# A spectral filter and MLP kernel: the second transform step over pairs of groups, on array quarters

## The chip, the cores and the metric

The kernel runs on one core of one Trainium2 chip. The metric is device time in microseconds (us) of one execution. Engines are named as the profile names them: PE is TensorE's matmul, PEld its weight load, DVE is VectorE, ACT is ScalarE, POOL is GpSimd, SP is SyncE (which issues the DMAs here).

## The reference

Four layers on an activation x of 2048 rows by 640 columns, in fp32: a spectral filter, an MLP over the rows, and both again.

```python
x = x + _A_ref(_layernorm(x), A_w_r, A_w_i)
x = x + _B_ref(_layernorm(x), B_w1, B_b1, B_w2, B_b2)
x = x + _A_ref(_layernorm(x), A_w_r, A_w_i)
x = x + _B_ref(_layernorm(x), B_w1, B_b1, B_w2, B_b2)

def _A_ref(x, w_r, w_i):            # x: (1, 2048, 640), w: (2048, 321)
    X = rfft2(x, axes=(-2, -1)) * (w_r + 1j * w_i)
    return irfft2(X, s=(S, D), axes=(-2, -1))

def _B_ref(x, w1, b1, w2, b2):      # w1: (2048, 1728), w2: (1728, 2048)
    u = gelu(einsum("bsd,sf->bdf", x, w1) + b1)
    return (einsum("bdf,fs->bds", u, w2) + b2).transpose(0, 2, 1)
```

## The kernel before

Everything is one class, `Layers`, whose `run` calls for each of two rounds `a1` (filter, forward transform and product), `a2` (inverse transform, residual) and an MLP: `b1st` in the first round, `b2nd` in the second.

Nearly all matmuls are in fp16 at fp32-like precision: an operand is split into a high part (`h`, made on ACT by a copy to fp16) and a low part (`l`, what is left, mostly made on DVE). `mm3` issues three matmuls for one product: high by high, high by low, low by high.

The two-dimensional transform is done by tables. Along the 2048 rows it goes in two steps (2048 = 16 x 128). The first step over rows, `a0_s1f` or `a0_s1`, is done per row tile `j` of 16; its result is written by `a0_s1h` (ACT) and `a0_s1l` (DVE) into `s1h` and `s1l`, both [128, 80, 16, 8] fp16. In the first layer this is a stage of its own, which ends at some 60 us; in the second it runs beside the first MLP, with a tail `a0_tail` after the last row tile.

Then `a1` works on 16 groups `g` of 128 rows of frequencies, 321 columns each for real and imaginary part:

- `dstage(g)` (called D in the prediction): the transform along columns, with `s1h` and `s1l` as stationary operands and table `tD`. 24 matmuls of 160 or 161 columns for the first two groups, 16 for the others: these take the remainder of the columns from a tile `stk`, filled by DMA (`stack`) from a DRAM copy `rest` of a part of `s1h` and `s1l`.
- `psplit`: ACT makes `ph`, DVE `pl`, from PSUM.
- `s2stage(g)` (s2): the second step over rows, table `tS2` as stationary operand, [128, 128] fp16: 12 matmuls of 321 columns. The table is block-diagonal but for the order of its rows: rows of the input are ordered `j16 * 8 + c8`, and a row of `c8` feeds only the 32 outputs of slot `c8 // 2`.
- `product`: the spectrum times the filter's weights `w` (loaded by DMA, three buffers): DVE makes `ta` and `tb` from PSUM, POOL combines them into `ta`.
- `xsplit`: ACT makes `xh`, DVE `xl`, both scaled by `sx`, a scale per row that `scale_x` computes once, in the first layer, with two small matmuls and a chain of small DVE operations that ends in `ce`. `twice` then copies 63 columns to the tile's end, of `xh` on ACT and of `xl` on POOL.
- `is2stage(g)` (IS): the inverse of s2, 36 matmuls of 64 rows by 128 columns.
- `yevict` (ACT) writes two thirds to `Y` in fp32; `y2evict` (ACT) takes the last third to `yt`, and `y2split` makes `Y2h` and `Y2l` of it on POOL.

The order is written out by hand: `self.pin = True` keeps each engine (PE, DVE, ACT, POOL) to the order in which the program issues instructions, one iteration of the loop at line 584 for each group. In an iteration PE has D of group g+1, IS of g-3, s2 of g; DVE has the products of g-1, `pl` of g+1, `xl` of g-2. Iterations also carry parts of other stages: `wsplit` of the first MLP weight tile in quarters (ACT and DVE), its scan and scale, loads of `tDi`, `tIM` and the weights. The last two groups are issued after the loop, in thirds.

PSUM is one pool of four buffers of two banks each, [128, 2, 512] fp32, handed out in turn by `big()`.

In `b1st` the second product accumulates, for each row tile `j` of 16, over 14 tiles of the 1728 hidden rows. The last hidden tile has 64 rows. It is stored twice in the 128 rows, and `ul` holds the high part in its lower half and the low part in its upper half, so that one matmul with `wh` does for two; the matmul with `wl` then takes 64 rows only:

```python
mm(o, wh[:, ft], ul[ft][:, a], start=False, stop=False)
mm(o, wl[:64, ft], uh[ft][:64, a], start=False, stop=True)
```

## Time and profile before

| | us |
|---|---|
| median of 3 runs | 1049.42 |
| lowest and highest | 1048.08, 1050.31 |
| the profiled execution's own time | 1049.02 |
| its span, first to last instruction | 1047.2 |
| PE busy in the span | 1003.6 |
| DVE busy | 710.7 |
| ACT busy | 586.0 |
| POOL busy | 273.1 |

The lines of the profile read as follows. A timeline row has the start in us from the span's start, the time taken, the engine, the line (L49 is the wrapper through which all pinned operations go, so operations are told apart by their tiles), the operation, the tiles written and read, and the shape; in brackets, the idle time before it and what ended it. Rows that follow closely may be merged (x2). A group row has the count, the busy time and the mean of one in ns, and the idle time before. A row of a tile has the shortest, the median and the longest duration in ns, then the first and the last start. A row by stretch has the stretch, its length, the busy time and count of PE, PEld, DVE, ACT and POOL, the granted TensorE clock (1.00 is full), the share of DMA and GB/s. The stages in order: first step over rows to about 60 us, first filter stage to 134.5, inverse to about 200, first MLP to 568, second filter stage from 576 to 649, then the inverse and the second MLP.

### The profile page before, as it was taken

How to read it: one execution, taken by the hardware profiler on the slowest of the kernel's cores; microseconds unless marked ns; L12 is line 12 of the kernel's file. 1: busy time of each engine (PE TensorE's matmuls, PEld its weight loads, DVE VectorE, ACT ScalarE, POOL GpSimd, SP SyncE). 2: the span in 40 equal slices, each digit the busy share in tenths (PEclk: the TensorE clock that was granted, in tenths of full speed). 3: DMA queues.
4: the chain of work that ended last, by engine and by line, in shares of the span. 5: the costliest groups of instructions: out<-in, count | busy, mean ns of one | idle time of the engine just before them, and what ended most of it. 6: DMA issues, size and time to landing. Idle time of an engine off the chain costs nothing.

```text
span 1047.2 us, 20920 instructions
## 1 busy us (share of the span) xinstructions
PE 1003.6 (96%) x8315; PEld 732.1 (70%) x8315; DVE 710.7 (68%) x1437; ACT 586.0 (56%) x910; POOL 273.1 (26%) x481
## 2 busy tenths in 40 slices
PE   4889989999999999999998998999999999999998
PEld 3778756677777776777775786666777777777776
DVE  7978947854333955666665797677655574987885
ACT  5857669765555555555542475894644454644532
POOL 6927867300000002211122487770000000000000
PEclk9589989999999999999999998999999999999999
DMA  7864336622222264444423543464422232445511
GB/s 224 311 204 127 99 116 200 205 86 83 82 82 77 71 239 139 131 122 129 126 87 110 171 119 111 130 196 172 132 95 81 74 107 92 137 140 180 165 44 51
DMA packets 55305, 137.38 MB, mean 131 GB/s; under 512 B 6540, under 2 KB 12328, under 8 KB 55208
## 3 DMA queue, kind: packets, MB, share of 16 engines
q1 hardware_dynamic: 55208, 136.06, 41.1%
q8 instruction: 65, 1.06, 0.4%
q14 instruction: 32, 0.26, 0.1%
HBM read 112.96 MB, written 23.07 MB: 130 GB/s over the span
## 4 chain that ended last, share of the span: by engine, by line
PE 85%; DVE 8%; POOL 2%; DMA 2%; ACT 1%; issue 1%; SPq 0%; POOLq 0%; ACTq 0%; DVEq 0%
PE ps L49 85%; DVE f L49 2%; DVE s1l L49 1%; DVE hl L49 1%; DVE st L49 1%; DVE ta L49 1%; DVE xt L49 1%; DVE xl L49 1%; DMA xt<-x 1%; POOL eo L49 1%; DVE wl L49 0%; POOL ta L49 0%; DMA rest<-s1l 0%; DMA raw<-w 0%; DVE tb L49 0%
## 5 line engine op out<-in xcount | busy, mean ns | idle before, releaser
L49 PEld LDWEIGHTS <-wh 128*128 128x128 f16 x2992 | 289.9, 98 | 115.9 <-issue 2.0
L49 PEld LDWEIGHTS <-wl 128*128 128x128 f16 (+1 forms) x1616 | 157.8, 98 | 67.1 <-issue 4.2
L49 PE MATMUL ps<-hh,wh 128*128 128x320 f16 x896 | 186.3, 299 | 0.8 <-ACT hh L49 0.8
L49 PE MATMUL ps<-hl,wh 128*128 128x320 f16 x896 | 184.7, 299 | 0.0
L49 PE MATMUL ps<-hh,wl 128*128 128x320 f16 x832 | 171.4, 299 | 0.1
L49 DVE SCALAR_TENSOR_TENSOR wl<-raw,s,wh 128x1024 f16<-128x1024 f32 (+2 forms) x88 | 103.6, 1181 | 87.3 <-ACT wh L49 87.2
L49 PE MATMUL ps<-uh,wl 128*128 128x320 f16 x448 | 134.2, 300 | 0.0
L49 PE MATMUL ps<-ul,wh 128*128 128x320 f16 x448 | 133.7, 299 | 0.0
L49 ACT ACTIVATE wh<-raw,s 128x1024 f16<-128x1024 f32 (+2 forms) x92 | 94.8, 1048 | 67.7 <-PE ps L49 61.7
L49 PE MATMUL ps<-uh,wh 128*128 128x320 f16 x416 | 124.3, 299 | 0.0
L49 POOL TENSOR_TENSOR r<-v,mh 128x1 f32<-128x1 f32 x64 | 35.7, 559 | 330.1 <-DVE nm L49 314.6
L49 ACT ACTIVATE junk<-raw 128x896 bf16<-128x896 f32 (+1 forms) x60 | 59.6, 994 | 47.5 <-DMA raw<-w 47.3
L49 DVE TENSOR_TENSOR xt<-xt,ps 128x320 f32<-128x320 f32 (+1 forms) x96 | 44.9, 490 | 40.9 <-ACT ec L49 25.8
L49 PE MATMUL ps<-u,wo 128*128 128x320 f16 x504 | 69.9, 299 | 0.0
L49 DVE TENSOR_TENSOR f<-eo 128x256 f32<-128x256 f32 (+1 forms) x128 | 40.0, 366 | 41.8 <-POOL eo L49 41.2
L49 PEld LDWEIGHTS <-wo 128*128 128x128 f16 x504 | 49.3, 98 | 19.1
L49 DVE BATCH_NORM_STATS2 st<-xt 128x6 f32<-128x320 f32 x128 | 56.2, 481 | 5.0 <-DMA xt<-x 4.9
L49 PE MATMUL ps<-tM,f 128*128 128x128 f32 x160 | 40.5, 436 | 19.1 <-DMA xt<-x 11.8
L49 ACT ACTIVATE z<-xt,nb,r 128x640 f32<-128x640 f32 x31 | 28.5, 919 | 54.1 <-POOL z L49 43.7
L49 POOL TENSOR_TENSOR eo<-z 128x320 f32<-128x320 f32 x63 | 54.2, 881 | 17.0 <-ACT z L49 15.1
L49 PE MATMUL ps<-tDi,yh 128*128 128x322 f16 x256 | 56.6, 312 | 1.6 <-ACT yh L49 1.6
L49 PE MATMUL ps<-ph,tS 128*128 128x321 f16 (+2 forms) x288 | 57.9, 286 | 0.0
(165 smaller groups left out, 1904.3 us busy)
## 6 DMA issues: line engine op xcount, KB each, us to landing
raw<-w SPq DMA_DIRECT2D x56, 512.0 KB
xt<-x SPq DMA_DIRECT2D x80, 320.0 KB
w<-w SPq DMA_DIRECT2D x48, 321.0 KB
x<-xt SPq DMA_DIRECT2D x48, 320.0 KB
raw<-w SPq DMA_DIRECT2D x32, 448.0 KB
raw<-w2z SPq DMA_DIRECT2D x32, 448.0 KB
out<-xt SPq DMA_DIRECT2D x15, 320.0 KB
stk<-rest SPq DMA_DIRECT2D x42, 64.0 KB
```

The source lines that it names most:

```text
L49: i = f(*a, **k)
```

## The change

The second step over rows takes groups in pairs. The input rows are reordered to `c8 * 16 + j16`, which makes `tS2` block-diagonal in two blocks of 64. For the first 14 groups (`PG`), a product of 128 rows is replaced by one of the 64 rows of a half: `s2pair` issues, for a pair, 48 matmuls of 64 x 64 by 321 columns, four in a row on the four quarters of the array, for groups `e` and halves `r`. The result of half `r` of both groups lies in one PSUM tile, so that a "group" after s2 is now half of each of two old ones; `k_rows`, `gsel` and the places in `Y` follow. Group 14 still goes by `s2stage`, group 15 in thirds.

With it the loop goes by pairs, the splits are shared out anew (the scale `sx` moves into the product; ACT copies to `xh`; `xl` is made half on DVE and half on POOL; the copies to the tail columns go to DVE; `Y2h` goes from POOL to ACT), PSUM is split into three buffers and one, `w` gets a fourth buffer, and `scale_x` and the scales use spare columns of a PSUM tile in use. In `b1st` the matmul with `wl` takes 128 rows, the upper half of `uh` being set to zero.

```diff
-    def big(self):
+    def big(self, one=None):
+        if one is None:
+            self.turn += 1
+            one = self.turn % 4 == 0
+        tag, bufs = ("one", 1) if one else ("big", 3)
         self.n += 1
-        return self.psum.tile([128, 2, 512], F32, tag="big", name=f"ps{self.n}")
+        return self.psum.tile([128, 2, 512], F32, tag=tag, name=f"ps{self.n}", bufs=bufs)
...
-        self.s1h = p.tile([128, 80, 16, 8], F16, name=f"s1h{self.n}")
-        self.s1l = p.tile([128, 80, 16, 8], F16, name=f"s1l{self.n}")
+        self.s1h = p.tile([128, 80, 8, 16], F16, name=f"s1h{self.n}")
+        self.s1l = p.tile([128, 80, 8, 16], F16, name=f"s1l{self.n}")
...
-        self.T.activation(self.s1h[:, :, j], pv, AF.Copy, scale=S1S / (zs * TS))
+        self.T.activation(self.s1h[:, :, :, j], pv, AF.Copy, scale=S1S / (zs * TS))
...
         def y2evict(g, ps):
+            y2hi(g, ps)
             yt = self.t(p, [128, 2, 32, 4], F32, "yt", 2)
             T.activation(yt, pairs(ps, 256, 384), AF.Copy, scale=YS)
             return yt
         def y2split(g, yt):
-            G.tensor_copy(y2[0][:, g], yt)
-            G.tensor_tensor(y2[1][:, g], yt, y2[0][:, g], op=ALU.subtract)
+            for q in range(2):
+                G.tensor_tensor(lanes(self.Y2[1], g)[:, q], yt[:, q], lanes(self.Y2[0], g)[:, q], op=ALU.subtract)
...
+        def xhi(g, c, x):
+            T.activation(xs[g % 3][0][:, :, c], x, AF.Copy)
+        def xlo(g, c, x, r=slice(0, 2), e=V):
+            xh, xl = (q[:, r, c] for q in xs[g % 3])
+            e.tensor_tensor(xl, x[:, r], xh, op=ALU.subtract)
...
+        def s2pair(u, x):
+            ps = self.big(False), self.big(True)
+            for a, b in ((0, 0), (1, 0), (0, 1)):
+                for ri in range(2):
+                    for q in range(2):
+                        for e in range(2):
+                            for r in range(2):
+                                m = slice(64 * r, 64 * r + 64)
+                                sp = 1 if u == e == r == 0 else 0
+                                mm(
+                                    ps[r][64 * e:64 * e + 64, ri, :NL], self.tS2[m, a, sp, 2 * ri + q, m],
+                                    x[e][b][m, q, :NL], start=a == b == q == 0, stop=b == q == 1,
+                                )
+            return ps
...
+        def times(o, ps, g, w, c=slice(0, NL)):
+            n = c.stop - c.start
+            V.scalar_tensor_tensor(
+                o, ps[:, :, c], self.sx[:, g:g + 1], w[:, c].unsqueeze(1).to_broadcast([128, 2, n]),
+                op0=ALU.mult, op1=ALU.mult,
+            )
+        def product(g, ps):
             ta, tb = (self.t(p, [128, 2, NL], F32, a, n) for a, n in (("ta", 3), ("tb", 2)))
+            times(ta, ps, g, w[g][:, 0])
+            times(tb, ps, g, w[g][:, 1])
             G.tensor_tensor(ta[:, 0], ta[:, 0], tb[:, 1], op=ALU.subtract)
+            gi = G.tensor_tensor(ta[:, 1], tb[:, 0], ta[:, 1], op=ALU.add)
+            if g + 4 < NG:
+                w[g + 4] = wload(g + 4)
+            return ta, gi
...
+        def xfinish(g):
+            xlo(g, whole, ta.pop(g), slice(0, 1))
+            xh, xl = xs[g % 3]
+            V.tensor_copy(xh[:, :, NL:], xh[:, :, 257:320])
+            V.tensor_copy(xl[:, :, NL:], xl[:, :, 257:320])
...
+        for i in range(NG // 2):
+            a, b, k = 2 * i, 2 * i + 1, 2 * i - 4
+            pa = dstage(a)
+            pa = phi(pa) if i else pquarters(pa)
+            if k >= 0:
+                pv[k] = is2stage(k)
+                evict(k)
+            if i:
+                ta[a - 2], _ = product(a - 2, ps2.pop(a - 2))
+                if k >= 0:
+                    y2split(k, yt.pop(k))
+            if k >= 0:
+                xfinish(k + 1)
+            pb = d = dstage(b)
+            pb = phi(pb) if i else pquarters(pb)
+            stack(2 * i + 4)
+            if i:
+                pa = plo(*pa)
+                xhi(a - 2, whole, ta[a - 2])
+            if k >= 0:
+                pv[k + 1] = is2stage(k + 1)
+                evict(k + 1)
+            if i:
+                ta[a - 1], gi = product(a - 1, ps2.pop(a - 1))
+                xlo(a - 2, whole, ta[a - 2], slice(1, 2), G)
+                pb = plo(*pb)
+            if i < NG // 2 - 1:
+                ps2[a], ps2[b] = s2pair(i, (pa, pb))
+            else:
+                ps2[a] = s2stage(a, *pa)
+            if k >= 0:
+                y2split(k + 1, yt.pop(k + 1))
...
+            if first and i == 0:
+                for _ in self.scale_x(p, d):
+                    pass
+            if i:
+                if i < NG // 2 - 1:
+                    xhi(a - 1, whole, ta[a - 1])
+                    xlo(a - 1, whole, ta[a - 1], slice(1, 2), G)
+                xfinish(a - 2)
...
+            for q in {4: (0, 1), 5: (2,), 6: (3,)}.get(i, ()):
+                self.wsplit(0, quarter(q)[0], lo=False, part=quarter(q)[1])
+            if i > 3:
+                self.wsplit(0, quarter(i - 4)[0], hi=False, part=quarter(i - 4)[1])
...
             if ft == NFT - 1:
                 V.tensor_copy(ul[ft][:64], uh[ft][:64])
+                G.memset(uh[ft][64:], 0.0)
...
                     mm(o, wh[:, ft], ul[ft][:, a], start=False, stop=False)
-                    mm(o, wl[:64, ft], uh[ft][:64, a], start=False, stop=True)
+                    mm(o, wl[:, ft], uh[ft][:, a], start=False, stop=True)
...
-            r_in = j16 * 8 + c8
+            r_in = c8 * 16 + j16
```

Here `pquarters` makes the first two groups' splits by halves (ACT, then DVE, for each half), `phi` and `plo` are the ACT and the DVE part of the old `psplit`, `evict` is `yevict` and `y2evict`, and `lanes` gives the places in `Y` and `Y2` of a group after s2.

More of the change, by code (lines that the diff above doesn't have):

```diff
@@ L34 @@
 YS = 2.0 ** -14
+PG = 14
 I32 = mybir.dt.int32
@@ L101, in setup @@
         base = self.base = self.push("base", side="left")
-        self.psum = self.push("ps", bufs=4, space=PSUM)
+        self.psum = self.push("ps", bufs=1, space=PSUM)
+        self.turn = 0
         self.dram = self.push("dr", space=DRAM)
@@ L1570, in k_rows @@
             out[g, s * 32 + 16:s * 32 + 32] = b
+    half = out[:PG].reshape(PG // 2, 2, 2, 64)
+    out[:PG] = half.transpose(0, 2, 1, 3).reshape(PG, 128).copy()
     return out
```

190 lines of the change are left out of this document (83 added, 107 removed).

## The prediction

> **What bounds the kernel now.** I read the page's part 1 first, then the busy time by stage, then the order of instructions on each engine inside the filter stage (the timeline), then the groups. Part 1 of the page:
>
> ```profile
> span 1047.2 us, 20920 instructions
> PE 1003.6 (96%) x8315; PEld 732.1 (70%) x8315; DVE 710.7 (68%) x1437; ACT 586.0 (56%) x910; POOL 273.1 (26%) x481
> ```
>
> PE bounds the whole, but the shares average over stages. Busy time by stretch (PE, PEld, DVE, ACT, POOL): two stretches of the first filter stage, one of the first MLP.
>
> ```profile
> 80.00:88.00 8.00, 8.00 (x134) 6.57 (x130) 7.06 (x9) 6.21 (x15) 6.72 (x10) 1.00 0.42 121
> 112.40:121.00 8.60, 8.60 (x146) 6.87 (x142) 8.60 (x11) 5.89 (x13) 7.93 (x12) 1.00 0.55 156
> 330.00:560.00 230.00, 230.00 (x1777) 162.83 (x1776) 146.67 (x387) 119.62 (x174) 37.12 (x87) 1.00 0.39 126
> ```
>
> In the MLP (third row) PE has no gap and the rest lie well below it. The filter stage is another matter: per 8.00 us, which is two groups, DVE has 7.06 and POOL 6.72; where DVE also splits weights (second row), DVE is full. Time taken from PE there is worth at most what those two leave. PE's order within one group:
>
> ```profile
> 84.54 0.31 PE L49 MATMUL ps<-ph,tS 128*128 128x321 f16 x1
> 86.20 0.30 PE L49 MATMUL ps<-tD,s1h 128*128 128x160 f16 x2
> 87.44 0.28 PE L49 MATMUL ps<-tI,xh 64*128 64x128 f16 x4
> 88.55 0.31 PE L49 MATMUL ps<-ph,tS 128*128 128x321 f16 x1
> ```
>
> Second step (s2) 1.66, the next group's first step (D) 1.24, inverse step (IS) 1.11: 4.01 us. s2's pace, 0.138 for 321 columns, would give 55 ns for the 128 columns of an IS matmul of 64 rows; the 36 of them take 31 ns each, so two halves of the array do run side by side.
>
> DVE and POOL hold each other up. One group where DVE is full, and one xl that POOL left alone:
>
> ```profile
> 108.80 0.81 DVE L49 SCALAR_TENSOR_TENSOR pl<-ps,ph 128x642 f16<-128x642 f32 x1
> 109.53 0.74 DVE L49 SCALAR_TENSOR_TENSOR wl<-raw,s,wh 128x512 f16<-128x512 f32 x1
> 110.19 1.38 DVE L49 SCALAR_TENSOR_TENSOR xl<-ta,sx,xh 128x642 f16<-128x642 f32 x1
> 121.99 0.88 DVE L49 SCALAR_TENSOR_TENSOR xl<-ta,sx,xh 128x642 f16<-128x642 f32 x1
> ...
> 108.95 0.76 POOL L49 TENSOR_TENSOR ta<-ta,tb 128x321 f32<-128x321 f32 x1 [0.26 <-DVE tb L49]
> 109.67 1.21 POOL L49 TENSOR_TENSOR ta<-tb,ta 128x321 f32<-128x321 f32 x1
> 110.82 0.99 POOL L49 CAST Y2h<-yt 128x256 f16<-128x256 f32 x1
> ```
>
> The xl takes 1.38 and not 0.88, the second ta 1.21 and not 0.76; pl, which reads PSUM, is undisturbed. Read as a lock taken in turn between POOL and any DVE operation with two SBUF inputs, and held for some 0.15 to 0.18 less than the duration, the rows fit: wl frees it at 110.13; ta runs 0.75 from there to 110.88 and frees it at 110.70; xl runs 0.88 from there, to 111.58.
>
> **The change, part by part.** *MLP tile.* The end of one output tile on PE:
>
> ```profile
> 466.94 0.30 PE L49 MATMUL ps<-uh,wl 128*128 128x320 f16 x1
> 467.08 0.30 PE L49 MATMUL ps<-ul,wh 128*128 128x320 f16 x1
> 467.31 0.31 PE L49 MATMUL ps<-uh,wl 64*128 64x320 f16 x1
> ...
> 468.03 0.28 PE L49 MATMUL ps<-tM,fh 128*128 128x128 f16 x2
> ```
>
> Within one size a step is 0.14. From 467.08 to 468.03 lie four steps of 0.237, each into another size: a switch costs 0.10. At 128 rows none is left: 4 x 0.10 x 16 tiles = -6.5 us, where PE has no gap. The new memset of uh's upper half runs on a POOL that idles there, during the earlier matmuls of the first tile; uncovered it would cost its own length, once.
>
> *PE in the filter.* Per pair s2 goes from 24 matmuls to 12 steps of four quarters, 3.3 to 1.65 us, if the quarters run side by side as the halves of IS do. D and IS stay at 4.7, switches go from four to five: about 6.5 us a pair, not 8.0. PE alone would give -1.5 x 14 = -21 us; DVE and POOL decide what arrives.
>
> *DVE and POOL per pair.* The durations used:
>
> ```profile
> L49 DVE SCALAR_TENSOR_TENSOR xt<-ps,c,xt 128x640 f32<-128x640 f32 x16 | 14.1, 882 | 8.7 <-ACT xt L49 4.3 <-PE ps L49 4.2
> L49 DVE TENSOR_TENSOR fs<-f,fs 128x320 f32<-128x320 f32 x14 | 6.8, 488 | 0.2
> L49 DVE COPY f<-eo x32: 168/169/722, 12.5 to 573.2; 128x2 f32<-128x2 f32 x32
> 12.30 1.68 POOL L49 TENSOR_TENSOR eo<-z 128x320 f32<-128x320 f32 x2
> 132.41 0.72 POOL L49 TENSOR_TENSOR Y2l<-yt,Y2h 128x256 f16<-128x256 f32 x1
> L49 POOL TENSOR_TENSOR yl<-Y,yh 128x512 f16<-128x512 f32 x30 | 34.8, 1160 | 10.9 <-ACT yh L49 10.9
> ```
>
> The products now multiply by sx as well: 0.88 each, the next start 0.80 later (0.07 more than now). The V half of xl takes 0.49. The two tail copies take 0.2 each, an estimate from 0.17 for two elements. One copy of two elements took 0.72: the first, at 12.5, beside POOL's eo of 12.30. So copies queue for the lock too. POOL, by the line through 0.72 at 256 and 1.16 at 512: 0.84 for the G half of xl, 0.50 for each y2 half; the Y2h cast and the tail copy leave it. ACT loses the tail copy and gains Y2h (0.38, below): still some 6.4 a pair.
>
> The order matters more than the sums. Let T be the end of a pair's second product on DVE. POOL does both ta from T+0.07 to T+1.77 (the V half of xl takes a turn in between), then the G half of xl, to T+2.54. Only then may DVE copy xl's tail: the wait that the change adds. Behind it on DVE stand the next pair's products. POOL's first y2 half slips in ahead (T+2.48 against the copy's T+2.61), so the copy runs at T+2.82 and the next product from T+2.92 to T+4.60. Then V half and two copies alternate with ta (to T+5.6), then pl (to T+6.35) and the second product: T+8.03. The second copy and the second ta ask within 0.02 us of each other; if the copy loses, T+8.6. I take 8.2, between the two and nearer to the order as worked out. Now it is 8.0. s2 is no bound: it starts at T+0.1, ends by T+2.0 and is needed at T+2.9. PSUM neither: the second IS waits for pl's buffer until T+6.5 and ends by T+7.7, before the next s2 can start.
>
> *DMA.* w loads gain a buffer and go out a group earlier; stk still goes out a whole pair ahead; the weight and table loads move by a group at most. Queues are idle enough (DMA share 0.42 above): nothing, or the few tenths of a late stk.
>
> *Sum over the stages.* Rows of DVE that mark the end of pairs 0, 1 and 6 now, in the first layer and the second, the first product after them, and the scale of x (xq, ce):
>
> ```profile
> 66.24 0.39 PE L49 MATMUL ps<-eye,xq 128*16 128x128 f32 x2
> 68.93 0.17 DVE L49 TENSOR_REDUCE ce<-cx 128x1 f32<-128x16 f32 x1
> 72.69 0.81 DVE L49 TENSOR_TENSOR tb<-ps,w 128x642 f32<-128x642 f32 x1
> 79.13 0.82 DVE L49 TENSOR_TENSOR tb<-ps,w 128x642 f32<-128x642 f32 x1
> 120.53 0.81 DVE L49 TENSOR_TENSOR tb<-ps,w 128x642 f32<-128x642 f32 x1
> 123.40 0.83 DVE L49 TENSOR_TENSOR ta<-ps,w 128x642 f32<-128x642 f32 x1 [0.54 <-PE ps L49]
> 587.29 0.82 DVE L49 TENSOR_TENSOR tb<-ps,w 128x642 f32<-128x642 f32 x1
> 594.08 0.81 DVE L49 TENSOR_TENSOR tb<-ps,w 128x642 f32<-128x642 f32 x1
> 635.08 0.81 DVE L49 TENSOR_TENSOR tb<-ps,w 128x642 f32<-128x642 f32 x1
> ```
>
> Fill, first layer: s2 of pair 0 now also waits for group 1's split, four halves of some 0.5 on ACT and DVE in turn, which puts xq and ce 1.5 later. The products now need that scale: from 70.6 product, pl, product end at 74.6, now 73.5. Pair 1 follows 7.9 later (now 6.45): +2.5. Second layer, where stk's landing holds both kernels: +1.2. Five pairs: 5 x 8.2, three weight splits of 0.66, and in the first layer 1.0 for the weight scale: 44.0 against 41.4, and 43.0 against 41.0, so +2.6 and +2.0. Drain: the next product starts 3.6 after pair 6 (handoff and the fourth split), now 2.1; the six small products cost 0.06 more each; POOL has one y2 split (1.1) less left, ACT three Y2h (1.1) more: +1.6 each. Filter: +6.7 and +4.8. With -6.5 that is +5.0 on the profiled execution's 1049.02 us, which lies 0.4 below the median of 1049.42: **1054**.
>
> *Strided writes.* s1h and s1l are now written one f16 in every 32 bytes, not in runs of eight. Nothing in this trace strides so. Rows to bound it:
>
> ```profile
> 63.48 0.50 DVE L49 SCALAR_TENSOR_TENSOR pl<-ps,ph 128x321 f16<-128x321 f32 x1 [2.29 <-ACT ph L49]
> 133.82 0.38 ACT L49 ACTIVATE Y2h<-ps 128x256 f16<-128x256 f32 x1
> 131.79 0.38 ACT L49 ACTIVATE yt<-ps 128x256 f32<-128x256 f32 x1 [0.53 <-POOL Y2l L49]
> 41.26 0.82 DVE L49 SCALAR_TENSOR_TENSOR s1l<-ps,s1h 128x640 f16<-128x640 f32 x1
> 44.26 0.82 DVE L49 SCALAR_TENSOR_TENSOR s1l<-ps,s1h 128x640 f16<-128x640 f32 x1
> ```
>
> Below: nothing (Y2h in runs of four f16 costs what dense yt costs; a gain is excluded, since both layouts move the same elements). Above: a second step per element. pl's 0.50 for 321 and 0.81 for 642 give 1.0 ns an element, so s1l would cost 0.64 more. In the first stage DVE has no gap and s1l comes every 3.00 us: 16 x 0.64 = +10, and the second layer's tail adds some 1; between them the MLP hides it. I take nothing, as the nearest row, Y2h, says, and keep +11 as an end.
>
> The Trainium skill, "SBUF — State Buffer", Door 1, speaks against that choice: full bandwidth needs at least two consecutive hits on a 16-byte line, and these writes make one. It gives no size; by it the upper end would be the likelier, 1065 and not 1054. The Y2h row makes four hits a line, so it agrees and doesn't test it.
>
> **The rivals.** *Strides cost*: 1054 + 11 = 1065; for and against, as above. *The quarters run two at a time*: s2 takes 3.3, ends at T+3.6 and holds the next product 0.7, so 7 x 0.7 x 2 = +10: 1064. For it: no matmul here splits the array's columns. Against: the rows split well. The Trainium skill, "TensorEngine Tiling (Array Packing)", section Tiling Modes, has four independent 64x64 tiles; its Restrictions and Gotchas say that column tiling turns fast weight load off, which no run here shows.
>
> *The other side, faster*: the tail copies do not queue for the lock (126 f16 elements, not two strided f32). Then xl's copy runs at T+2.61, no turn is lost, and a pair takes 7.4. First layer +2.1 fill, -1.3 pairs, +1.4 drain; second +0.7, -2.0, +1.4; with -6.5 that is 1045. It decides below 7.7 us a pair. *The gains cancel*: the handoff at 8.0 and a drain that POOL's lighter load shortens, filter +6: 1049.
>
> **How the numbers follow.** A measurement of this kernel can tell 0.2%, 2 us, from no change. Handoff with 8.0 to 8.6 us a pair: 0.40, own range 1050 to 1059, 0.07 of it within 0.2%. Strides 0.16 and quarters 0.07, both slower. Copies without the lock 0.28, faster. Cancelled 0.09, same. Faster 0.28, same 0.16, slower 0.56. The range 1042 to 1065 leaves out the better half of the faster case's spread, and prices that come together.
>
> **What would show it.** MLP: no 64x320 rows, steps of 0.14 throughout. s2: 64x321 matmuls, four in 0.14 us. Handoff: DVE idle for some 0.8 us before a copy of 126 elements, released by POOL's xl; PE with gaps; every second tb 8.0 to 8.6 after the last but one. Strides: s1l at 0.82 or at 1.45. The prediction is wrong if pairs come under 7.7 us, or if s1l is slow.

## The result, and the profile after

The changed kernel takes **1141.2 us** (median; before 1048.8): ratio 1.088, 95% interval 1.086 to 1.090. The direction of the forecast was right, its size was not: 1054, with a range up to 1065. First the page of the changed kernel, its first part.

```profile
span 1139.7 us, 21688 instructions
PE 1009.5 (89%) x8651; PEld 739.1 (65%) x8651; DVE 776.2 (68%) x1491; ACT 648.9 (57%) x914; POOL 269.5 (24%) x482
```

The span is 92.5 longer, but PE is busy only 6 us longer; DVE and ACT gained 65 and 63 us of work. The groups of the changed kernel say which (count, busy us, mean ns of one, idle time before them):

```profile
L50 ACT ACTIVATE s1h<-ps 128x640 f16<-128x640 f32 x31 | 90.9, 2942 | 1.3 <-PE ps L50 1.2
L50 DVE SCALAR_TENSOR_TENSOR s1l<-ps,s1h 128x640 f16<-128x640 f32 x31 | 89.8, 2920 | 21.4 <-ACT s1h L50 21.2
```

`s1l` took 0.82 in the rows of before and takes 2.92; `s1h` does as badly. That is 4.6 ns an element. The upper bound that I had set was 1.45 for an `s1l`, which is 2.3 ns an element.

The stages, each from PE's first matmul of its kind to the next stage's (first D; first inverse with `tDi`; first matmul with `uh`; first D of the second layer; first `tDi` again; PE's end), in us, for the main kernels below:

| | first step | filter 1 | inverse, MLP 1st product | MLP 2nd product, tail | filter 2 | rest |
|---|---|---|---|---|---|---|
| before | 60.4 | 74.9 | 235.9 | 204.7 | 74.5 | 393.3 |
| changed | 80.1 | 90.5 | 237.8 | 250.3 | 83.5 | 394.0 |
| before, strided writes | 79.9 | 80.8 | 234.7 | 249.4 | 76.0 | 393.6 |
| changed, runs of four | 59.0 | 85.0 | 236.4 | 202.4 | 81.4 | 394.4 |
| the same, own tails | 59.3 | 81.3 | 235.6 | 203.8 | 74.8 | 394.3 |
| before, MLP edit | 60.3 | 76.2 | 235.9 | 200.7 | 75.0 | 393.3 |
| four buffers (last one below) | 59.5 | 77.6 | 235.4 | 200.2 | 73.2 | 394.4 |

So the loss lies in the first step (+19.7), in the MLP's second product, beside which the second layer's first step runs (+45.6), and in the filters (+15.6, +9.0). Busy time by stretch in the changed kernel (PE, PEld, DVE, ACT, POOL, then clock, DMA share, GB/s): one stretch in the first step, and one of seven row tiles in the MLP:

```profile
30.00:75.00 45.00, 26.41 (x103) 23.17 (x103) 44.66 (x86) 43.92 (x59) 22.90 (x54) 0.50 0.59 196
479.10:589.70 110.60, 91.23 (x687) 64.76 (x686) 68.08 (x156) 62.08 (x71) 18.10 (x42) 0.92 0.33 101
```

In the first step DVE and ACT are both full; an `s1l` comes every 4.5 us there, not every 3.0. In the MLP nothing is full: DVE 62%, ACT 56%, and PE, which had no gap before, 82%. What holds it is seen in DVE's order, from one `xt` (the row tile's sum, which reads PE's result out of PSUM) to the next (timeline of the changed kernel):

```profile
479.10 0.88 DVE L50 SCALAR_TENSOR_TENSOR xt<-ps,c,xt 128x640 f32<-128x640 f32 x1
...
481.74 0.88 DVE L50 BATCH_NORM_STATS2 st<-xt 128x6 f32<-128x320 f32 x2
484.37 2.88 DVE L50 SCALAR_TENSOR_TENSOR s1l<-ps,s1h 128x640 f16<-128x640 f32 x1 [1.75 <-ACT s1h L50]
...
488.14 0.14 DVE L50 TENSOR_SCALAR nm<-mv 128x1 f32<-128x1 f32 x1
...
491.87 1.03 DVE L50 TENSOR_TENSOR f<-eo 128x64 f32<-128x64 f32 x4 [2.52 <-POOL eo L50]
...
493.91 0.82 DVE L50 TENSOR_TENSOR fl<-f,fh 128x640 f16<-128x640 f32 x1 [0.80 <-ACT fh L50]
...
494.93 0.88 DVE L50 SCALAR_TENSOR_TENSOR xt<-ps,c,xt 128x640 f32<-128x640 f32 x1
```

DVE takes its operations in this order, and the waits between them are for other engines that in turn waited for DVE: `xt`, statistics, `nm`, then (on POOL and ACT) `r`, `z`, `eo`, then `f`, `fh`, `fl`, and only then the next row tile's `xt`. It is one serial chain, 15.83 us long, and the wait for the slow `s1h` (1.75) and the slow `s1l` sit in it. No `xt` waits for PE; PE, whose PSUM buffers are freed by `xt`, waits for it (timeline of the changed kernel):

```profile
527.43 0.16 PE L50 MATMUL ps<-sqb,ones 128*128 128x1 bf16 x1 [3.59 <-DVE xt L50]
...
527.68 0.47 PE L50 MATMUL ps<-ul,wh 128*128 128x320 f16 x1
527.95 0.47 PE L50 MATMUL ps<-uh,wl 128*128 128x320 f16 x1
```

These matmuls come 0.27 us apart, where they came 0.135 apart without such waits; this is why PE is busy for 91 us in the second stretch, with 84 us of work at the faster pace (7 row tiles of 12.00, as measured below with the MLP edit alone). It is not what holds the stage, since no `xt` waits for PE.

The filter's own steps came as the prediction has them (timeline of the changed kernel; the last number is idle time and its cause):

```profile
127.24 1.29 PE L50 MATMUL ps<-ph,tS 64*64 64x321 f16 x31 [0.15 <-DVE tb L50]
128.24 0.84 PE L50 MATMUL ps<-pl,tS 64*64 64x321 f16 x16
...
124.69 0.18 DVE L50 COPY xl<-xl 128x126 f16<-128x126 f16 x1
128.35 0.74 DVE L50 COPY xh<-xh 128x126 f16<-128x126 f16 x1
129.83 0.43 DVE L50 COPY xl<-xl 128x126 f16<-128x126 f16 x1 [0.74 <-POOL xl L50]
...
128.04 1.00 POOL L50 TENSOR_TENSOR ta<-tb,ta 128x321 f32<-128x321 f32 x1
129.00 0.80 POOL L50 TENSOR_TENSOR xl<-ta,xh 128x321 f16<-128x321 f32 x1
```

Of a pair's 48 small matmuls 47 take 1.78 us, to the next D at 129.02: four quarters do run side by side. DVE stands idle 0.74 until POOL's half of `xl` is done. Copies of 126 elements take 0.18 or 0.74: the `xh` copy at 128.35 began while POOL was at an operation, and ended (129.09) when that did (129.04); the `xl` copy at 124.69 began together with POOL's next operation (124.68).

### The profile page after: what moved, and what is told of

Its sections match the earlier page's. It is cut to its first block, busy times and chain, and to the rows that moved or that the text cites. A ratio compares the mean times of both kernels' runs of the same rounds, so it can differ in the third digit from the quotient of the medians.

```text
span 1139.7 us, 21688 instructions
## 1 busy us (share of the span) xinstructions
PE 1009.5 (89%) x8651; PEld 739.1 (65%) x8651; DVE 776.2 (68%) x1491; ACT 648.9 (57%) x914; POOL 269.5 (24%) x482
## 4 chain that ended last, share of the span: by engine, by line
PE 52%; DVE 23%; ACT 12%; issue 5%; DMA 4%; POOL 4%; SPq 0%; POOLq 0%; ACTq 0%; DVEq 0%
PE ps L50 52%; DVE s1l L50 8%; ACT s1h L50 3%; ACT wh L50 3%; DMA xt<-x 3%; DVE wl L50 2%; DVE ta L50 2%; DVE f L50 2%; DVE tb L50 2%; POOL eo L50 2%; DMA raw<-w 2%; ACT junk L50 1%; ACT z L50 1%; DVE pl L50 1%; DVE xl L50 1%
## 5 line engine op out<-in xcount | busy, mean ns | idle before, releaser
L50 PEld LDWEIGHTS <-wh 128*128 128x128 f16 x2992 | 293.2, 99 | 149.6 <-issue 33.4
L50 PEld LDWEIGHTS <-wl 128*128 128x128 f16 x1616 | 159.5, 99 | 64.1 <-DVE wl L50 0.5
L50 DVE SCALAR_TENSOR_TENSOR wl<-raw,s,wh 128x1024 f16<-128x1024 f32 (+2 forms) x88 | 106.2, 1211 | 89.3 <-ACT wh L50 89.2
L50 PE MATMUL ps<-uh,wh 128*128 128x320 f16 x416 | 129.5, 311 | 10.6 <-DVE mv L50 10.6
L50 PE MATMUL ps<-ul,wh 128*128 128x320 f16 x448 | 138.2, 310 | 0.0
L50 PE MATMUL ps<-uh,wl 128*128 128x320 f16 x448 | 138.2, 310 | 0.0
L50 DVE SCALAR_TENSOR_TENSOR s1l<-ps,s1h 128x640 f16<-128x640 f32 (+2 forms) x33 | 92.5, 2854 | 21.4 <-ACT s1h L50 21.2
L50 ACT ACTIVATE s1h<-ps 128x640 f16<-128x640 f32 (+2 forms) x33 | 94.0, 2876 | 2.6 <-PE ps L50 2.5
L50 DVE TENSOR_TENSOR f<-eo 128x256 f32<-128x256 f32 (+1 forms) x128 | 34.5, 330 | 41.9 <-POOL eo L50 41.3
L50 PEld LDWEIGHTS ps<-tM,f 128*128 128x128 f32 x160 | 35.0, 312 | 41.8 <-DVE f L50 41.3
```

What stands on the lines that cost most here:

```text
L50: i = f(*a, **k)
```

## The experiments

**Which part costs.** Theory A: the single f16 in every 32 bytes. Rivals: the new split of PSUM or PE's clock (B), any layout with less than 16 bytes in a row (C). First the changed kernel with another order of rows, which keeps the two 64-row blocks and writes runs of four (here and below a part of the edit; `s1l` and the views of both change alike):

```diff
-        self.s1h = p.tile([128, 80, 8, 16], F16, name=f"s1h{self.n}")
+        self.s1h = p.tile([128, 80, 2, 16, 4], F16, name=f"s1h{self.n}")
...
-            r_in = c8 * 16 + j16
+            r_in = c8 // 4 * 64 + j16 * 4 + c8 % 4
```

> The changed kernel, with only the order of the rows in s1h and s1l (and the rows of table tS2 that go with it) altered: c8//4*64 + j16*4 + c8%4, so that each write makes runs of four f16 (8 bytes) instead of one f16 in every 32 bytes. The two 64-row blocks of tS2 and the quarters stay. Theory A (the step of 32 bytes between single f16 elements is what costs): s1h falls from 2.94 us to about 0.7, s1l from 2.92 to about 0.8; the first stage ends near 61 us and not 84, the first MLP's second product takes some 190 us (195.9 before less 6.5) and not 230, the tail after it 9.4 and not 23; only the filter's own loss is left (13.0 and 6.6, of which the prediction had 6.7 and 4.8), less 6.5 in the MLP: 1048.8 + 13.0 + 6.6 + 2 - 6.5 = 1064, or 1056 if part of the filter's loss came from the late first stage. Theory B (the first stage and the MLP lose by the new split of PSUM into three buffers and one, or by PE's clock): s1h and s1l may fall, but the MLP's second product keeps 220 us or more and the time stays above 1100. Theory C (any layout with less than 16 bytes in a row costs): s1l stays above 1.2 us and the time lies between 1075 and 1100.

Measured 1065.7, ratio 1.016 (1.014 to 1.018). Groups of this kernel:

```profile
L50 DVE SCALAR_TENSOR_TENSOR s1l<-ps,s1h 128x640 f16<-128x640 f32 x31 | 25.1, 813 | 0.2 <-ACT s1h L50 0.2
L50 ACT ACTIVATE s1h<-ps 128x640 f16<-128x640 f32 x31 | 21.4, 690 | 8.2 <-PE ps L50 8.1
```

Both are back at their old durations, and 75.6 of the 92.5 us are gone. Then the other way round, the strided layout alone in the kernel before:

```diff
-        self.s1h = p.tile([128, 80, 16, 8], F16, name=f"s1h{self.n}")
+        self.s1h = p.tile([128, 80, 8, 16], F16, name=f"s1h{self.n}")
...
-            r_in = j16 * 8 + c8
+            r_in = c8 * 16 + j16
```

> The kernel before, with one thing of the change: s1h and s1l as [128, 80, 8, 16], written one f16 in every 32 bytes, and the rows of tS2 ordered c8*16 + j16 to match. The second step stays whole (128 x 128), groups stay single, PSUM stays one pool of four. Theory A: s1h and s1l take 2.9 us each as in the changed kernel; the first stage +22, the MLP's second product +34.3 + 6.5 (what the MLP edit gives elsewhere) = +41, its tail +13: 1048.8 + 76 = 1125. Theory B (PSUM split, clock): s1h and s1l slow but the MLP hides most: under 1090. If the writes are slow only beside the changed kernel's other work: 1049.

Measured 1119.7, ratio 1.067 (1.065 to 1.068): +70, with 2.9 us for each write and nearly the whole loss of the first step and of the MLP (table). Of the 5.9 in its first filter most are the writes' too (timeline of this kernel):

```profile
83.40 0.31 PE L49 MATMUL ps<-tD,s1l 128*128 128x160 f16 x1 [3.07 <-DVE s1l L49]
83.51 0.47 PE L49 MATMUL ps<-tD,s1h 128*128 128x160 f16 x2
```

D waits 3.07 for the last `s1l` (0.54 before), and after that idle time PE runs for 5 us at half its pace: a pair of such matmuls takes 0.27 from start to next start, 0.14 before. The wait is 2.5 longer, and the slow pace costs some 2.5 more. Theory A holds; B falls, and so does C, by the kernel with runs of four.

**The price by itself.** A kernel of writes and reads only, 640 elements per partition:

> Leaves the whole computation out and measures the disputed price by itself, on tiles of 128 x 640: first ACT alone writes 640 f16 from PSUM with a step of 2, 4, 8, 16, 32 and 64 bytes between elements, six times each (actw1x to actw32x), then f32 elements at a step of 32 bytes (actf8x), f16 at 32 bytes from SBUF, and reads f16 at these steps with a dense write (actdense); then DVE alone writes at 2 to 32 bytes (dvew1x to dvew16x), and reads its second input at 2 to 64 bytes with a dense write (dvedense); then POOL writes at 2 and at 32 bytes; then ACT and DVE write at 32 bytes at the same time; then ACT at 32 bytes beside DVE dense. Theory P (a lone write has a price of its own): as soon as an element has no written neighbour the write takes some 4.6 ns whatever the step: 2.9 us from 4 bytes on, on both engines, reads at 0.7 to 0.85 throughout. Theory S (the price grows with the bytes stepped over): 0.7 at 4 and 8 bytes, 1.5 at 16, 2.9 at 32, 5.9 at 64. Theory 32 (the step must be a multiple of 32 bytes to be slow): 0.7 up to 16 bytes, 2.9 at 32 and 64. Theory C (ACT and DVE slow each other): 0.7 to 1.5 alone, 2.9 only in the stretch where both write. Theory R (the strided read of s1h is part of it on DVE): dvedense rises with the step.

Its groups; `actw8x` is ACT's write at a step of 8 elements (16 bytes), `actf8x` the same in f32 (32 bytes), `dvedense<-ps,actw8x` a dense write that reads its second input at that step.

```profile
L49 ACT ACTIVATE actw16x<-ps 128x640 f16<-128x640 f32 x30 | 85.4, 2847 | 32.3 <-DVE dvew16x L49 31.8
L49 ACT ACTIVATE actw8x<-ps 128x640 f16<-128x640 f32 x6 | 18.1, 3012 | 0.2
L49 ACT ACTIVATE actw32x<-ps 128x640 f16<-128x640 f32 x6 | 18.0, 2993 | 0.2
L49 DVE SCALAR_TENSOR_TENSOR dvew16x<-ps,actdense 128x640 f16<-128x640 f32 x6 | 17.2, 2862 | 0.2
L49 POOL TENSOR_TENSOR poolw16x<-src,dvedense 128x640 f16<-128x640 f32 x6 | 17.2, 2862 | 0.4
L49 ACT ACTIVATE actw4x<-ps 128x640 f16<-128x640 f32 x6 | 9.5, 1582 | 0.2
L49 POOL TENSOR_TENSOR poolw1x<-src,dvedense 128x640 f16<-128x640 f32 x6 | 8.4, 1392 | 228.3 <-DVE dvedense L49 227.9
L49 ACT ACTIVATE actf8x<-ps 128x640 f32<-128x640 f32 x6 | 8.2, 1366 | 0.2
L49 DVE SCALAR_TENSOR_TENSOR dvedense<-ps,actw8x 128x640 f16<-128x640 f32 x6 | 7.6, 1271 | 0.2
L49 ACT ACTIVATE actw2x<-ps 128x640 f16<-128x640 f32 x6 | 5.3, 878 | 0.2
L49 DVE SCALAR_TENSOR_TENSOR dvedense<-ps,actw4x 128x640 f16<-128x640 f32 x6 | 4.9, 824 | 0.2
L49 ACT ACTIVATE actw1x<-ps 128x640 f16<-128x640 f32 x6 | 4.2, 703 | 2.7 <-DVE ps L49 2.6
```

No theory had it whole. The price grows with the step (0.70 dense, 0.88 at 4 bytes, 1.58 at 8, 3.0 at 16), as theory S has it in kind, but it is reached at half the steps that S named; from 16 bytes on it stays (2.85, 2.99), as theory P says. Counted by 16 bytes touched it is nearly one price: 5.5 ns at a step of 4 bytes (160 lines of 16 bytes), 4.9 at 8, 4.7 at 16, 4.4 at 32. One engine alone pays it, so theory C of this run falls. Reading at a step of 16 bytes costs DVE 0.45 us beside a dense write (R), but an `s1l` that both reads and writes with a step of 32 bytes takes no longer (2.91 in the kernel before with strided writes) than the write alone (2.86). ACT and DVE took turns where they were meant to write at the same time, so whether they slow each other is not measured. An f32 element alone in its 32 bytes pays 2.1 ns, half of what an f16 pays, which suggests that a lone write of less than 4 bytes is what is dear. Runs of two test that (the changed kernel with `s1h` as `[128, 80, 4, 16, 2]` and rows ordered `c8 // 2 * 32 + j16 * 2 + c8 % 2`):

> As the kernel with runs of four, with runs of two f16 (4 bytes, every 64 bytes): rows ordered c8//2*32 + j16*2 + c8%2. With theory P, one price of some 4.6 ns per run of neighbours and not per element: 320 runs make s1h and s1l 1.5 us each, against 0.69 and 0.81 for runs of four (160 runs, 0.74 at that price) and 2.9 for single elements. In the first stage, where DVE has no gap, 16 x 0.7 = +11 on the 1065.7 of runs of four, and some 2 to 3 in the tail after the MLP: 1078. With theory S or 32 (step in bytes): 64 bytes is at least as slow as 32, so half the elements' price, the same 1.5, or more: up to 2.9 and 1120. If only an element alone is slow and a pair of f16 (4 bytes) is a full write: 0.7 to 0.8 and 1066.

Measured 1062.7, ratio 1.011 (1.010 to 1.013): no slower than runs of four. Groups of this kernel:

```profile
L50 DVE SCALAR_TENSOR_TENSOR s1l<-ps,s1h 128x640 f16<-128x640 f32 x31 | 25.1, 813 | 0.2 <-ACT s1h L50 0.2
L50 ACT ACTIVATE s1h<-ps 128x640 f16<-128x640 f32 x31 | 22.0, 710 | 9.7 <-PE ps L50 9.5
```

A pair of f16 in every 64 bytes costs no more than a dense row; one price for every run, which theory P took, is refuted. A pair pays at most 2.2 ns (0.71 us for 320), as an f32 does; the single f16 in its own 16 bytes, whose neighbour in the same 4 bytes is not written with it, pays 4.4 and more. Why is not shown.

**The MLP edit alone**, in the kernel before:

```diff
-                    mm(o, wl[:64, ft], uh[ft][:64, a], start=False, stop=True)
+                    mm(o, wl[:, ft], uh[ft][:, a], start=False, stop=True)
```

> The kernel before, with the MLP edit alone: the matmul with wl of the last hidden tile takes 128 rows, and POOL sets the upper half of that uh to zero. Prediction's term: four switches of 0.10 us in each of 16 row tiles, -6.5 us: 1042.3. Rival: the switch is paid elsewhere (a 128-row matmul of 0.14 in place of one of 64 rows that the profile shows at 0.31 for two): no change, 1048.8.

Measured 1046.4, ratio 0.9965 (0.9953 to 0.9977): -3.4, half. PE's work in the stage did fall by 6.3 (199.96 to 193.69), and PE went from row tile to row tile in 12.00 us without a gap, where it took 12.42 before. But the `xt` come no closer than this (timeline of this kernel, with PE's last matmul of the second product and the last `xt`):

```profile
423.85 0.88 DVE L49 SCALAR_TENSOR_TENSOR xt<-ps,c,xt 128x640 f32<-128x640 f32 x1
435.99 0.89 DVE L49 SCALAR_TENSOR_TENSOR xt<-ps,c,xt 128x640 f32<-128x640 f32 x1
...
561.68 0.30 PE L49 MATMUL ps<-uh,wl 128*128 128x320 f16 x1
564.53 0.88 DVE L49 SCALAR_TENSOR_TENSOR xt<-ps,c,xt 128x640 f32<-128x640 f32 x1
```

The same two rows at the end of the stage in the kernel before:

```profile
567.10 0.31 PE L49 MATMUL ps<-uh,wl 64*128 64x320 f16 x1
567.45 0.88 DVE L49 SCALAR_TENSOR_TENSOR xt<-ps,c,xt 128x640 f32<-128x640 f32 x1 [3.06 <-PE ps L49]
```

DVE's chain takes 12.14 a row tile in both kernels. In the kernel before it is 0.28 below PE, makes up what it was late at the start, and at the end waits 3.06 for PE. With the edit it is 0.14 above PE, and the last `xt` comes 2.55 after PE's last matmul has ended (561.98). The next stage starts 8.5 after the last `xt` in both, so 2.5 of the 6.3 are lost there.

**Does that chain set the stage?** First I tried to shorten it, which failed. The stage is ordered by a planner (the software that sets the order where `self.pin` does not), not by the program. In the changed kernel, `f`, `fh`, `fl` were issued an iteration later in the program:

> The changed kernel, writes of single f16 every 32 bytes and all, with one thing altered in the first MLP's second product: of a row tile's chain to the first step over rows (statistics, z, eo, f, fh, fl), the last part (f, fh, fl) is issued an iteration later, after the next row tile's sum with xt. Chain theory: in that stage no engine is full (DVE is busy 62% before), but each engine's order makes one serial chain per row tile, xt, statistics, r, z, eo, f, fh, fl and then the next xt; it takes 12.14 us a row tile in the kernel before, where PE takes 12.42, and 15.8 with slow s1h and s1l, which sit in it. Cut, the stage goes back to PE's pace though the writes stay slow: 230 falls to some 195, and the time to 1141 - 35 = 1106; the first stage and the tail keep their losses. Rival (the stage is bound by DVE's or ACT's own busy time, or by PSUM's new split): 15.8 a row tile stays, 1141.

This gave 1138.2, with most row tiles still 15.8 apart: in the trace these operations stand in their old place. Next the order was forced (issued after the next `xt`):

> The changed kernel, slow writes and all, with the chain of the MLP's second product really cut. The kernel meant to do so only altered the program's order; that stage is ordered by a planner, which put f, fh and fl back in their old place (a row tile still took 15.8). Here f, fh and fl of row tile j-1 are made to be issued after row tile j's sum with xt. Chain theory: then DVE no longer waits for eo and fh between one xt and the next. From one xt to the next DVE still has s1l behind ACT's wh and s1h, and the z and fh of ACT: 15.8 less the 1.9 of eo, the idle 2.5 before f and 0.8 before fl, some 12 to 13 a row tile; the stage falls from 230 to 195 to 205 and the time to 1105 to 1115, with s1h and s1l at 2.9 as they were. Rival (busy time or PSUM binds): 15.8 stays and the time with it.

This gave 1148.5, with row tiles about 17.6 apart: `xt` now stood behind a weight scan, for which DVE waited 4.4 us (for ACT's `junk`, itself late from a DMA of weights). The expected 12 to 13 was wrong, and so was the rival's 15.8. The same work in another order is slower by 2 us a tile, so busy time is not what counts. The same two edits in the kernel before, together with the MLP edit:

> The kernel before with the MLP edit and the same cut of the chain in the MLP's second product. The MLP edit alone gave -3.4 of the -6.5 that PE's rows promise. Chain theory: PE then needs 12.0 a row tile and the chain 12.14, so the chain took the rest back (a row tile took 12.14, and the tail after the last one 11.0 and not 8.5); cut, the whole 6.5 shows and the tail is at 8.5 or less: 1042 to 1043. Rival (the loss is elsewhere, PE's clock or a switch that remains): 1046 stays.

> The kernel before with the MLP edit and the order really cut as above. Chain theory: the chain falls below PE's 12.0 a row tile, so PE's pace shows: in steps of 12.0 and not 12.14, and no PE wait but the start of the tail. The whole 6.5 of the edit and perhaps the tail's extra 2.5: 1041 to 1043. Rival (what the edit lacks is elsewhere): 1044 to 1046.

The first gave 1043.9, ratio 0.995 (0.994 to 0.997): 2.5 less than the MLP edit alone, though steady row tiles are still 12.14 apart; two early ones came faster (11.4 and 11.5), and the last `xt` is 1.25 behind PE and not 2.55. The forced order gave 1047.6, worse than either forecast, with row tiles 11.8 to 14.5 apart.

So I lengthened a link instead, first by a second `s1l` with the same values:

> The kernel before, where in the MLP's second product every s1l is written twice, the second time with the same values: one more DVE operation of 0.81 us per row tile, 0.73 in DVE's order, which the planner puts between wl and v. DVE is busy 62% in that stage. Chain theory: the operation lies in the serial chain from one xt to the next, 12.14 becomes 12.87 us a row tile, PE's 12.42 no longer sets the pace, and some 0.45 x 11 row tiles = +5 come out: 1053 to 1054, with row tiles 12.87 apart. Rival (busy time counts, and 4.5 us of DVE's 12.4 are idle): nothing, 1048.6, row tiles stay 12.14 to 12.4 apart.

It was swallowed: 1049.7, with row tiles 11.9 to 12.0 apart, no longer than before. In the planner's new order the wait of 0.69 for `wh` is gone, which makes up for the 0.73 that the operation takes. Five of them, and the next link kept behind the last:

```diff
-        self.a0_s1l(j, pv)
+        for _ in range(5):
+            self.lasts1 = self.a0_s1l(j, pv)
...
+                with self.after(*([self.lasts1] if self.lasts1 else [])):
+                    vn = self.stats3(p, mv, self.CA, self.CB)
```

> The kernel before, where in the MLP's second product every s1l is written five times with the same values, and v and nm, the next link towards z, are made to be issued on DVE after the last of them (the planner moved the second s1l of the earlier kernel in between and took a wait for wh out: row tiles stayed 11.9 to 12.0 apart). Four more operations are 2.9 us a row tile, 10.7 us of DVE's work in 12.4: not full. Chain theory: row tiles come 11.94 + 3 x 0.73 = 14.1 to 14.6 apart in place of 12.14, PE waits for them, and with PE's 12.42 that is 1.7 to 2.2 for each of 11 or 12 row tiles: +19 to +26, 1067 to 1075. Rival (busy time counts, DVE has room for them): 1049 to 1051, row tiles 12.4 apart at most.

Measured 1078.8, ratio 1.027 (1.025 to 1.030). Timeline of this kernel, and its busy time in that stretch:

```profile
469.68 0.88 DVE L49 SCALAR_TENSOR_TENSOR xt<-ps,c,xt 128x640 f32<-128x640 f32 x1
484.20 0.88 DVE L49 SCALAR_TENSOR_TENSOR xt<-ps,c,xt 128x640 f32<-128x640 f32 x1
```

```profile
424.00:542.00 118.00, 105.83 (x817) 72.94 (x816) 84.08 (x212) 55.67 (x82) 20.70 (x48) 1.00 0.34 108
```

14.52 apart, as the chain theory has it, with DVE at 71%: the rival (room on DVE hides it) falls. A chain of DVE's that is longer than PE's row tile sets this stage. The total is 4 us over the expected 1067 to 1075: from PE's last row tile to the next stage it takes 21.2 us in place of 8.5, more than I had counted.

**The pair loop.** To see what the handoff costs, the kernel with runs of four was given tails copied by the engine that made the rest of the row. The tail of `xh` thus goes from DVE to ACT, and DVE waits for no result of POOL's there:

```diff
             e.tensor_tensor(xl, x[:, r], xh, op=ALU.subtract)
+            if r != slice(0, 2):
+                xl = xs[g % 3][1][:, r]
+                e.tensor_copy(xl[:, :, NL:], xl[:, :, 257:320])
...
+        def htail(g):
+            xh = xs[g % 3][0]
+            T.activation(xh[:, :, NL:], xh[:, :, 257:320], AF.Copy)
...
-            V.tensor_copy(xh[:, :, NL:], xh[:, :, 257:320])
-            V.tensor_copy(xl[:, :, NL:], xl[:, :, 257:320])
```

> The kernel with runs of four, and besides the handoff from POOL to DVE taken out of the pair loop: the tail of xh is copied on ACT right after xh, and each half of xl has its tail copied by the engine that made it (DVE its half, POOL its half), so that DVE waits for no POOL result there. Handoff theory (the wait of 0.74 to 0.8 per pair, the xh copy of 0.74 that queues for the lock, and the turns lost to it set the pair): a pair falls from 9.05 to 8.0 or less where DVE splits weights and from 8.0 to 7.4 where not, 12 us less than the kernel with runs of four over both layers, so some 1048 to 1052. Rival (DVE's and POOL's own work and the lock set the pair, and the wait is slack that moves elsewhere): 0.3 a pair, 4 us less. Second rival: POOL, which takes on a copy of 0.15 to 0.29 per group, becomes the bound: no change or slower.

Measured 1054.3, ratio 1.005 (1.003 to 1.007): -11.4 on runs of four. Every second `tb` marks a pair; first with runs of four, then with own tails (timelines):

```profile
603.53 0.88 DVE L50 SCALAR_TENSOR_TENSOR tb<-ps,sx,w 128x642 f32<-128x642 f32 x1
...
611.68 0.87 DVE L50 SCALAR_TENSOR_TENSOR tb<-ps,sx,w 128x642 f32<-128x642 f32 x1
```

```profile
600.39 0.87 DVE L50 SCALAR_TENSOR_TENSOR tb<-ps,sx,w 128x642 f32<-128x642 f32 x1
...
607.46 0.88 DVE L50 SCALAR_TENSOR_TENSOR tb<-ps,sx,w 128x642 f32<-128x642 f32 x1
```

8.15 us a pair, and 7.07 without the handoff and with the `xh` copy (0.74) off DVE; the run does not part the two. Next, what the quarters bring: the second step at half rate (128 rows by 64 columns, two side by side).

> The kernel with runs of four, with the second step over rows at half its rate: 48 matmuls of 128 rows (half of them zeros of the table) by 64 columns, two side by side, instead of 48 of 64 by 64, four side by side. All else stays. It measures what the quarters bring. The prediction's reading (PE is not the bound of the pair loop; s2 starts 0.1 after T and is needed at T+2.9): s2 goes from 1.78 to some 3.4 and ends at T+3.5, 0.6 too late in each of 7 pairs and 2 layers: +8, 1074. Rival (the slack is larger than that): within 2 us of 1065.7. Rival (PE sets the pair): 1.65 a pair, +23, 1089.

Measured 1072.8, ratio 1.021 (1.020 to 1.023), +7.2 on runs of four. PE's second step now takes 3.75 a pair (timeline of this kernel):

```profile
613.21 2.71 PE L50 MATMUL ps<-ph,tS 128*64 128x321 f16 x32
615.73 1.29 PE L50 MATMUL ps<-pl,tS 128*64 128x321 f16 x16
```

That is 2.0 more than 1.78, and 7 pairs in two layers would be 27 us were PE the bound. It is not: pairs without a weight split went from 8.15 to 8.46, those with one stayed at 9.1. Most of the loss is in the first pairs of each filter stage, where a product on DVE waits once for the second step (1.93 and 2.60 us; 0 and 1.23 with the quarters). The expected +8 was close, but by another sum: 0.6 in every pair had been forecast.

**A version that beats both.** Two waits of the kernel with own tails (timeline):

```profile
87.01 0.16 DVE L50 TENSOR_REDUCE sqb<-sq 128x1 bf16<-128x2 f32 x1 [2.96 <-ACT junk L50]
...
428.94 0.16 PE L50 MATMUL ps<-sqb,ones 128*128 128x1 bf16 x1 [3.78 <-DVE xt L50]
```

One edit spreads the scan over two pairs, lets the weight splits on DVE lag a pair, and gives the small matmul (`sqb`) a spare column of a PSUM tile in use:

> The kernel with runs of four and own tails, with two waits more taken out that its trace shows. First, in the MLP's second product the small matmul that sums a weight tile's squares takes no PSUM buffer of its own but a spare column of the row tile before (it waited 3.8 us for a buffer once, 2.9 in the kernel with runs of four). Second, in the filter each weight split on DVE follows its split on ACT one pair later (the last one goes to the start of the inverse stage), and the scan of the first weight tile is spread over two pairs with its scale two pairs on (DVE waited 1.72 for wh and 2.96 for the scan). By the waits: -3.8 in the MLP, -1.7 in each filter stage and -2.5 in the first: 1054.3 - 9.7 = 1044.6, which is 5 below the kernel before. Rival (the waits move: ACT is late with ph in the same pairs, and the inverse stage pays for the fourth split): 1050, no better than before.

1048.4, ratio 0.999 (0.997 to 1.000): the filters gained (75.8 and 73.3), but the spare column belongs to the row tile that `xt` has yet to read, so the wait stayed (2.9). Next, with buffers of its own again for that matmul, the MLP's program order altered as above, and then with the order forced:

> Runs of four, own tails, splits and scan a pair later (as in the kernel at 1048.4), the sums of squares again in PSUM buffers of their own, and the chain in the MLP's second product cut. Of the 1048.4, 2.9 was one wait of PE for a row tile's sum with xt, which comes an f, fh, fl earlier now, and PE's pace of 12.0 counts instead of the chain's 12.14: some 5 off, 1043. Rival (waits for buffers move to the s1 tiles, which come an iteration later): 1048.

> Runs of four, own tails, splits and scan a pair later, and the order in the MLP's second product really cut. Against 1048.6 with the order not cut, where PE waited 2.9 once for a row tile's xt and the row tiles went at 12.14: by the chain theory 12.0 a row tile and no such wait, some 4 to 6 off: 1043 to 1045, no better than the kernel before with the MLP edit alone. Rival: 1048.

These gave 1048.6 and 1051.4, not the 1043 to 1045 that was hoped for: in the first of them the wait was still there (4.2). At last the first of the two with PSUM as one pool of four buffers outside the filter:

> Runs of four, own tails, splits and scan a pair later, the program's order altered in the MLP as in the kernel at 1048.6, and PSUM again one pool of four buffers outside the filter stage (three and one only inside it). With three and one, PE waited once in the MLP's second product for a row tile's xt (4.2 us) and ran 0.3 us a matmul and more slowly after it; the kernel before with the same MLP had no such wait. If the split does it: 4 to 5 off, 1043.5 to 1044.5, the same as the kernel before with MLP edit and altered order (1043.9), for the mended filter takes 1.1 less over both layers. Rival (the planner's order does it, not the buffers): 1048.

1044.4, ratio 0.995 (0.993 to 0.996), as expected, and without that wait: the split had caused it. This version is 0.5% faster than the kernel before, and so beats both. But so is the kernel before with the MLP edit and the altered program order (1043.9), which has no paired filter. The pairs add nothing to that: the two filter stages take 77.6 and 73.2, against 74.9 and 74.5 in the kernel before. The second filter stage, four buffers first, then before:

```profile
572.80:646.00 73.20, 62.46 (x1233) 52.98 (x1232) 60.87 (x96) 48.19 (x106) 53.10 (x95) 0.92 0.44 133
```

```profile
575.90:650.50 74.60, 68.10 (x1066) 55.67 (x1066) 60.68 (x84) 44.57 (x91) 51.94 (x82) 0.96 0.48 141
```

Here PE's work fell by 5.6 us and the time by 1.4; DVE and POOL have as much to do as ever.

## Why the prediction was wrong, and where it was right

- **Strided writes: the step that failed.** I took nothing for them, and +11 as an end. Measured: 75.6 between the changed kernel and the one with runs of four, 70 in the kernel before. Two parts of this term were mis-sized, the price of a write and the share of it that is hidden. The price: my upper end, a second step per element, is near what an f32 element (1.37) or a strided read (1.27) pays; a single f16 pays 2.9. The nearest row, `Y2h` in runs of four, was right about runs of four, as the experiment shows, and says nothing about single elements. Between ends that far apart the range should not have stopped at the one cost that I could name. The Trainium skill, "SBUF — State Buffer", Door 1, spoke against my choice: it has a penalty for each access that crosses to a new 16-byte line. For single f16 writes the trace agrees: the price levels off at a step of 16 bytes, from where each write has a line of its own. It does not agree that two hits on a line are enough: at a step of 8 bytes they are two, and 1.58 is over twice the dense 0.70. A pair side by side makes two hits as well, and there the trace agrees (0.71).
- **"Between them the MLP hides it": failed too.** I read hiding from busy shares (DVE 146.67 of 230), as if 4.5 us of each row tile were free. The stage had a chain of 12.14 us a row tile beside PE's 12.42, so only 0.28 a tile could be hidden. The slow writes made the chain 15.83, and the stage lost 45.6.
- **MLP tile, -6.5:** the switches cost what I said (PE's work fell 6.3), but the end came only 3.4 earlier. Some 2.5 of the rest went into the same chain, which was now the slower one; I had named no next limit.
- **Handoff: right** for a pair without a weight split: taken at 8.2, it is 8.15, idle 0.74 for 0.8. The copies do wait for POOL, so the faster rival, which let them through, fell.
- **Fill and drain:** within 0.7 but for one. The fill is +2.8 and +2.7 (taken +2.5 and +1.2), the drain +2.3 and +1.6 (taken +1.6 each); all with runs of four, against before.
- **Five pairs, +2.6 and +2.0:** +5.1 and +2.5. A weight split costs 0.9 a pair, not 0.66, and the pair with the weight scan takes 10.1, not 9.2, since DVE waits 1.74 for ACT's scan.
- **Quarters: right**, 1.8 against 1.65; the rival (two at a time) fell.
- **PSUM: right in the filter**, where with runs of four a product on DVE waited for PE only once, in the second layer's fill. **Beyond it the prediction did not look**, and there the split costs one wait of 3 to 4 us.

With the writes mended, the prediction would have stood at +5 against a measured +15.9. Of the difference 5.5 come from the filters, 4.1 from the MLP, 1.3 from elsewhere. So it was slower than forecast even apart from the failed step, and that the direction was right owes most to a cost that was taken at nothing. The last version's 1044.4 is the faster rival's 1045 in number only: it needed own tails, three waits fewer and another order in the MLP.

## What to carry to other kernels

Before a layout is turned, look at what each write leaves beside it: pairs of f16 cost as little as a dense row here, one f16 alone in its 16 bytes four times that on ACT, 3.5 times on DVE. A stage where PE has no gap is not proof that the other engines have room: follow one period of the second engine's order, from an operation to the same one in the next tile, and compare its length with PE's. A chain that is 0.28 us a tile below PE can hide 0.28 us a tile and no more, and when PE is made faster than the chain, the chain sets the end.

## What was not expected of the hardware

- Single f16 writes: 0.70 us dense, 0.88 at 4 bytes, 1.58 at 8, 3.0 at 16 and no more beyond, for 640 elements on ACT; the same on DVE (2.86 at 32) and, from a dense 1.39, on POOL (2.86).
- Pairs of f16 every 64 bytes cost no more than dense; an f32 alone every 32 bytes 1.37; reads of f16 on DVE nothing up to 8 bytes, and 0.4 to 0.5 us more (1.27 for 0.82 at 16 bytes) from 16 bytes on.
- A copy of 126 elements on DVE that began while POOL was at an operation took 0.74 and ended with POOL's; one that began together with POOL's next operation took 0.18.
- After 3 us of idle time PE took 0.27 for two matmuls of 160 columns in place of 0.14, for some 5 us, while the granted clock reads 1.00 in that stretch (kernel before with strided writes).
